# Fewer, wider filler products in the opening of a fused attention and gated feed-forward kernel

## The chip, the cores and the metric

The kernel runs on one core of a Trainium2 chip. The metric is device time in microseconds (us) of one execution; the kernel before takes 227.95 us (median of 8 runs, 227.79 to 228.54).

## The reference, cut to what matters

For each of 8 batches there are x (8 heads, 512 rows, 64 columns) and a state (8 heads, 32 rows, 64 columns). They attend to each other, the results are put together to 544 rows of 512 per batch, and all rows go through a gated feed-forward layer.

```python
scores  = scale * x @ state.T;  a  = softmax(scores);  xread = a  @ state   # per batch, per head
scores2 = scale * state @ x.T;  a2 = softmax(scores2); sread = a2 @ x
x = concatenate([xread, sread], axis=2)        # heads side by side: (8*544, 512)
gate = maximum(x @ w_gate, 0)                  # (512, 1536)
val  = x @ w_val
out  = (gate * val) @ w_out                    # (1536, 512)
```

## The kernel before, in words

Matrix products are in bf16 with sums in fp32. The kernel never forms xread: since xread = a @ state, the product x @ w_gate is a @ (state @ w_gate). So for each batch b it makes U = state @ w_gate and state @ w_val (128 x 1536 for each half of the heads and each weight), and then multiplies U by the transposed probabilities ANS.

The work of a batch runs over these helpers. The name that the program text uses for each stands in front.

- **dx, dw, do, ds, df** load x, the gate and value weights, the output weight, the rest of the state and a raw x. All of these are issued on POOL's queue (L95 to L112, L418). A `dw.w.lo.n` loads columns lo to lo+n of weight w (0 gate, 1 value).
- **stc, stT, sto**: the state is converted (L119, L122), transposed on TensorE (L127) and copied out of PSUM to stT (L131).
- **xc, xT, xo** (batch 0) and **xT2, xo2** (batches 1 and 2): x is converted to xb (L144), transposed on TensorE (L167, L171, L184) and copied to xT (L175, L187). The first half of batch 0 comes in fp32 over SyncE's and ScalarE's queues and is converted on VectorE; its other half and batches 1 and 2 are converted by POOL's DMA on the way.
- **sc, ex, nr, nx**: scores (L198), exponential (L205), sum and reciprocal (L211, L213), scaling to a_sn (L217).
- **aT, ao**: a_sn is transposed (L233) and copied to ANS (L247).
- **c, co** and **u, uo**: pieces of U, on TensorE (L289) and copied out (L309, L299).
- **gv, re, mu**: gate and value for 128 columns (L314), relu (L338), product (L342) to h_sb.
- **o, of**: output products (L351), copy and store (L359).
- **sr, sn**: the other attention's read (L262).

The code is scheduled by hand (`manual_schedule`): each engine does its instructions in the order of the calls. For the opening, some 55 us, that order is a text, `program` (L440 on), of words such as `xT2.1.1@2`: the helper, its arguments, and after @ the numbers of the PSUM banks that it writes. After it, loops over g (batch and block of 128 columns) issue gv, relu, mult and output pieces, with the work of later batches hung on fixed places.

PE (TensorE) has words of its own in the text, `spin`: filler products whose result, in bank 7 (`warm_ps`), nothing reads. Their operands are 512 zero columns of hs_sb, which is not used until the end; VectorE clears them first (L394).

```python
def spin(n, cols=512):
    for i in range(n):
        nc.tensor.matmul(warm_ps[:, 0:cols], warm[:, 0:128], warm[:, 0:cols], start=True, stop=True)
```

There are nine groups in the opening: ahead of stT.0, of xT.0.1, of sc.0.0, of xT.0.2, of sc.0.1, of xT2.1.1, of sc.1.0, of c.1.0.128 and of c.0.128.128. A filler waits for no engine but for the first clearing; it lies in PE's order, so what follows it can't start until it is through. The first wide products, gv.0.0, come after the last group.

Of the kernel before, what the change touches and what calls it, by code (L numbers as in the profile page):

```python
# [16 lines left out]
def kernel(  # L17
# [52 lines left out]
    stT = const.tile([128, B, NJ, 64], BF16, name="stT")  # L70
# [5 lines left out]
    xf, xb, xT, e_sn, a_sn, ANS, U, hsb, sr_sb = {}, {}, {}, {}, {}, {}, {}, {}, {}  # L76
# [360 lines left out]
             "c": c_unit, "co": c_out, "u": u_unit, "uo": u_out, "gv": gv, "re": relu, "mu": mult, "o": out_part,  # L437
             "of": fin_x, "xn": x_next, "xp": x_pad, "sr": sr_mm, "sn": sr_norm}
    program = """
    dx.1.0.2 dx.1.1.2 stc.0.0.act stc.0.1.dve spin.23.128 stT.0@0 xc.0.0.dve dw.0.0.128 sto.0.act dw.1.0.128 on  # L440
    xc.0.1.dve spin.16.128 xT.0.1@1 dw.0.128.128 xT.0.0@2 xo.0.1.dve xo.0.0.act dw.1.128.128 spin.13.128 sc.0.0@3
    dw.0.256.256 ex.0.0 spin.4.128 xT.0.2@4 xT.0.3@5 xo.0.2.dve dw.1.256.256 xo.0.3.act nr.0.0 spin.13.128 sc.0.1@0
    dw.0.512.256 xT2.1.0@1 ex.0.1 nx.0.0 xo2.1.0.act nr.0.1 dw.1.512.256 spin.8.128 xT2.1.1@2 xo2.1.1.act spin.2.128
    sc.1.0@3 dw.0.768.256 nx.0.1 ex.1.0 dw.1.768.256 spin.10.128 c.1.0.128@45 c.0.0.128@01 co.1.0.128.0.dve aT.0.1@2
    co.0.0.128.0.act aT.0.0@3 co.1.0.128.1.dve co.0.0.128.1.act dw.0.1024.256 sc.1.1@4 ao.0.1.dve ao.0.0.act nr.1.0
    ex.1.1 dw.1.1024.256 spin.7.128 c.0.128.128@05 gv.0.0@12 co.0.128.128.1.act nr.1.1 co.0.128.128.0.act nx.1.0.pool
    re.0.0 gv.0.1@34 mu.0.0 re.0.1 nx.1.1.pool c.1.128.128@50 mu.0.1 co.1.128.128.1.act c.0.256.256@12
    co.1.128.128.0.act c.1.256.256@30 dw.0.1280.256 co.0.256.256.0.dve co.0.256.256.1.act aT.1.1@5 aT.1.0@4
    co.1.256.256.0.act co.1.256.256.1.dve dw.1.1280.256 gv.0.3@21 ao.1.1.act ao.1.0.dve dx.2.0.1 re.0.3 gv.0.2@30
    mu.0.3 ds re.0.2 c.1.512.256@54 mu.0.2 gv.1.2@21 co.1.512.256.1.act co.1.512.256.0.act do.0.6 c.0.512.256@30  # L450
    re.1.2 gv.1.5@45 co.0.512.256.0.dve xp.1 co.0.512.256.1.act mu.1.2 re.1.5 gv.1.3@23 mu.1.5 re.1.3 gv.1.1@04
    do.6.12 mu.1.3 re.1.1 c.1.768.256@15 xp.0 mu.1.1 gv.1.4@23 co.1.768.256.0.act co.1.768.256.1.act c.0.768.256@04
    re.1.4 gv.1.0@15 co.0.768.256.0.dve co.0.768.256.1.act df.3 mu.1.4 re.1.0 gv.1.6@20 mu.1.0 re.1.6 gv.0.4@41 mu.1.6
    re.0.4 gv.0.6@35 mu.0.4 re.0.6 gv.1.7@20 mu.0.6 re.1.7 c.0.1024.256@41 c.0.1280.256@35 mu.1.7 co.0.1024.256.0.act
    xT2.2.0@2 stc.1.0.pool co.0.1024.256.1.act co.0.1280.256.1.dve xT2.2.1@0 stc.1.1.pool co.0.1280.256.0.act
    xo2.2.0.dve gv.0.5@41 stc.3.0.pool stc.3.1.pool xo2.2.1.dve re.0.5 stc.2.1.pool gv.0.10@53 stc.2.0.pool mu.0.5
    re.0.10 stT.1@2 gv.0.9@40 mu.0.10 sto.1.act re.0.9 sc.2.1@1 gv.0.8@52 ex.2.1 mu.0.9 re.0.8 nr.2.1 gv.0.11@34
    re.0.11 mu.0.8 gv.0.7@10 nx.2.1.pool mu.0.11 re.0.7 sc.2.0@5 o.0.0@6 mu.0.7 ex.2.0 nr.2.0 c.1.1280.256@32
    c.1.1024.256@14 co.1.1280.256.1.act u.2.1.1024@50 o.0.1 co.1.1024.256.0.dve co.1.1024.256.1.act nx.2.0.pool
    uo.2.1.1024.1.dve uo.2.1.1024.0.act o.0.2 co.1.1280.256.0.act u.2.0.0@21 xn.3 of.0.0.dve u.2.1.0@45 uo.2.0.0.1.act  # L460
    u.2.1.512@03 uo.2.1.0.0.dve o.0.3@7 uo.2.1.0.1.act uo.2.0.0.0.dve uo.2.1.512.0.act aT.2.0@1 aT.2.1@4
    uo.2.1.512.1.dve ao.2.0.act o.0.4 ao.2.1.act o.0.5 gv.2.1@50 of.0.1.act re.2.1 gv.1.10@23 mu.2.1 re.1.10
    gv.1.11@14 mu.1.10 re.1.11 gv.2.3@50 mu.1.11 re.2.3 gv.2.2@23 mu.2.3 re.2.2 u.2.0.1024@14 u.2.0.512@50 mu.2.2
    uo.2.0.1024.1.act sr.0@2 o.0.6@6 uo.2.0.512.1.act uo.2.0.512.0.dve sn.0 gv.1.9@34 uo.2.0.1024.0.dve re.1.9
    gv.1.8@05 mu.1.9 re.1.8 gv.2.0@21 mu.1.8 re.2.0 o.0.7 mu.2.0 o.0.8 o.0.9@7 of.0.2.dve sr.1@3 sn.1 xp.2 xp.3
    """
    for word in program.split():
        word, _, banks = word.partition("@")
# [101 lines left out]
```

## Time and profile before

| | |
|---|---|
| median of 8 runs | 227.95 us |
| the profiled execution's own time | 227.82 us |
| span of its profile | 226.0 us |
| TensorE products busy | 220.6 us, 98% of the span |
| VectorE, ScalarE, GpSimd busy | 57%, 55%, 23% |
| fillers (L430) | 96 products, 9.3 us busy, 261 ns mean |
| gv products (L314) | 384, 96.6 us |
| output products (L351) | 372, 94.5 us |

The span is what the profiler saw of the engines' work; what lies around it makes the time longer by 1.8 us. PE is TensorE's product, PEld its weight load, DVE VectorE, ACT ScalarE, POOL GpSimd, SP SyncE. A product's duration contains the time that it takes to drain through the array, so products that overlap have a mean above their spacing: a row of output products says 379 ns, and they follow each other every 216 ns. Start times are in us from the start of the span. A DMA's time to landing counts from its issue.

### The profile page before, as it was taken

To read this page: it belongs to the slowest core of one execution; us is meant where nothing else is said; L and a number is where in the kernel's file an instruction comes from. 1 tells how busy PE (TensorE), PEld (TensorE's weight loads), DVE (VectorE), ACT (ScalarE), POOL (GpSimd) and SP (SyncE) were. 2 spreads that over 40 slices of the span, in tenths; PEclk is the share of its full clock that TensorE was granted. 3 is DMA by queue.
4 is the path that set the end of the run, shared out by engine and by line. 5 is a ranking of instruction groups with operands and counts; after the bars stand their busy time and mean duration, and the time that the engine had idled before them with its cause. 6 is when DMAs were issued, how large, how long until landed. Compare 5 with 4: busy or idle time off the path is not lost.

```text
span 226.0 us, 5017 instructions
## 1 busy us (share of the span) xinstructions
PE 220.6 (98%) x2040; PEld 110.8 (49%) x2040; DVE 128.4 (57%) x226; ACT 124.8 (55%) x236; POOL 53.1 (23%) x58
## 2 busy tenths in 40 slices
PE   7999999999999999999999999999999999999994
PEld 6964454444445444434434444344444445666543
DVE  3477888757478648763877467656855443222100
ACT  4489878865366654755556455555555444322221
POOL 8699838503333060006000600000000000000000
PEclk9999999999999999999999999999999999999999
DMA  6999999070719921691179113611311111111132
GB/s 147 178 195 196 213 227 273 27 186 3 208 70 133 252 85 46 139 278 50 49 97 260 69 62 75 142 46 46 96 46 49 46 48 46 48 51 76 62 94 95
DMA packets 37800, 25.50 MB, mean 113 GB/s; under 512 B 18864, under 2 KB 33200, under 8 KB 37776
## 3 DMA queue, kind: packets, MB, share of 16 engines
q1 hardware_dynamic: 24912, 16.85, 27.6%
q0 software_dynamic: 11968, 7.47, 21.4%
q10 hardware_dynamic: 896, 0.85, 1.3%
q8 instruction: 16, 0.26, 0.5%
q14 instruction: 8, 0.07, 0.1%
HBM read 18.35 MB, written 8.91 MB: 121 GB/s over the span
## 4 chain that ended last, share of the span: by engine, by line
PE 96%; DMA 1%; ACT 0%; issue 0%; DVE 0%; DVEq 0%; ACTq 0%
PE o_ps L351 38%; PE gv_ps L314 38%; PE gv_ps L331 5%; PE up L289 4%; PE warm_ps L430 2%; PE upc L289 2%; PE sc_ps L198 2%; PE sr_ps L262 1%; DMA st_f<-in_state_dram 1%; PE o_ps L377 1%; PE xT_ps L184 1%; PE aT_ps L233 1%; PE stT_ps L127 1%; PE srT_ps L275 0%; PE xT_ps L167 0%
## 5 line engine op out<-in xcount | busy, mean ns | idle before, releaser
L314 PE MATMUL gv_ps<-ans,U 128*128 128x512 bf16 x384 | 96.6, 380 | 0.0
L351 PE MATMUL o_ps<-wo_sb,h_sb 128*128 128x512 bf16 x372 | 94.5, 379 | 0.0
L342 DVE TENSOR_TENSOR h_sb<-gv_ps,g_sb 128x512 bf16<-128x512 f32 x96 | 65.3, 688 | 42.2 <-ACT g_sb L338 41.0
L338 ACT ACTIVATE g_sb<-gv_ps 128x512 bf16<-128x512 f32 (+1 forms) x108 | 63.0, 584 | 47.0 <-PE gv_ps L314 32.4
L351 PEld LDWEIGHTS <-h_sb 128*128 128x128 bf16 x372 | 36.0, 98 | 41.0 <-issue 0.7
L314 PEld LDWEIGHTS <-U 128*128 128x128 bf16 x384 | 34.8, 98 | 41.3 <-issue 4.2
L359 ACT COPY o_sb<-o_ps 128x512 f32<-128x512 f32 x29 | 17.0, 586 | 20.7 <-PE o_ps L351 20.7
L299 DVE CAST U<-up 128x512 bf16<-128x512 f32 x36 | 23.2, 685 | 5.3 <-PE up L289 5.2
L299 ACT CAST U<-up 128x512 bf16<-128x512 f32 x36 | 19.4, 592 | 10.1 <-PE up L289 10.1
L140 POOL CAST xb<-xf 128x1024 bf16<-128x1024 f32 x10 | 10.3, 1060 | 52.4 <-DMA xf<-in_x_dram 42.7
L254 POOL COPY xa<-xb 128x2048 bf16<-128x2048 bf16 (+1 forms) x9 | 15.3, 1711 | 13.9 <-issue 7.0
L211 DVE TENSOR_REDUCE cs<-e_sn 128x16 f32<-128x512 bf16 x16 | 10.9, 683 | 8.6 <-ACT e_sn L205 8.6
L342 DVE TENSOR_TENSOR hs_sb<-gv_ps,g_sb 128x256 bf16<-128x256 f32 x12 | 5.1, 425 | 15.3 <-PE gv_ps L331 10.5
L205 ACT ACTIVATE e_sn<-sc_ps 128x512 bf16<-128x512 f32 x16 | 9.6, 601 | 5.6 <-PE sc_ps L198 5.6
L430 PE MATMUL warm_ps<-hs_sb 128*128 128x128 bf16 x96 | 9.3, 261 | 1.5 <-DVE hs_sb L394 1.2
L309 ACT CAST U<-upc 128x512 bf16<-128x512 f32 (+1 forms) x20 | 9.5, 530 | 1.7 <-PE upc L289 1.6
L289 PEld LDWEIGHTS <-stT 64*32 64x32 bf16 x512 | 4.9, 89 | 10.6 <-issue 10.1
L430 PEld LDWEIGHTS <-hs_sb 128*128 128x128 bf16 x96 | 7.7, 121 | 2.0 <-DVE hs_sb L394 1.2
L217 DVE TENSOR_TENSOR a_sn<-e_sn,rc 128x512 bf16<-128x512 bf16 x12 | 8.3, 692 | 0.6
L331 PE MATMUL gv_ps<-br,wg_sb 128*128 128x256 bf16 x48 | 7.2, 273 | 0.0
L331 PE MATMUL gv_ps<-br,wv_sb 128*128 128x256 bf16 x48 | 7.2, 273 | 0.0
L289 PE MATMUL up<-wg_sb,stT 64*32 64x512 bf16 x144 | 7.2, 386 | 0.0
(64 smaller groups left out, 133.9 us busy)
## 6 DMA issues: line engine op xcount, KB each, us to landing
out_dram<-o_sb SPq DMA_DIRECT2D x31, 256.0 KB, 2.3
xf<-in_x_dram SPq DMA_DIRECT2D x4, 1024.0 KB, 6.2
wo_sb<-in_moe_w_out_dram POOLq DMA_DIRECT2D x2, 768.0 KB, 15.4
wg_sb<-in_moe_w_gate_dram POOLq DMA_DIRECT2D x5, 256.0 KB, 8.6
wv_sb<-in_moe_w_val_dram POOLq DMA_DIRECT2D x5, 256.0 KB, 9.2
xf<-in_x_dram POOLq DMA_DIRECT2D x1, 1024.0 KB, 16.0
xb<-in_x_dram POOLq DMA_DIRECT2D x3, 256.0 KB, 7.3
xb<-in_x_dram POOLq DMA_DIRECT2D x1, 512.0 KB, 12.0
```

Source lines behind the costliest of these rows:

```text
L140: copy[eng](out=xb[b][:, :, hs].rearrange("p c h d -> p h c d"), in_=xf[b][:, hs])
L211: nc.vector.reduce_sum(out=cs, in_=e_v, axis=AX.X)
L254: nc.gpsimd.tensor_copy(out=v[:, hs:hs + src.shape[1]], in_=src)
L289: nc.tensor.matmul(dst[parity][32 * j:32 * j + 32], stT[r:r + 64, b, j, 32 * parity:32 * parity + 32], wsb[r:r + 64, j, lo:lo + n], start= ...
L299: copy[eng](out=U[b][:, w, kc, lo:lo + 512], in_=held["u", b, w, lo][kc])
L314: nc.tensor.matmul(ps[w], U[b][:, w, kc, f0:f0 + 128], ANS[b][:, kc].rearrange("p c t -> p (c t)"), start=(kc == 0), stop=(kc == NK - 1))
L331: nc.tensor.matmul(ps[w][:, 0:nt], wsb[:, j, f0:f0 + 128], br[:, j].rearrange("p b n -> p (b n)"), start=(j == 0), stop=(j == NJ - 1))
L338: nc.scalar.activation(out=g_sb[:, 0:n], in_=ps[0][:, 0:n], func=AF.Relu)
L342: nc.vector.tensor_tensor(out=dst, in0=ps[1][:, 0:n], in1=held["g", b, jf][:, 0:n], op=ALU.mult)
L351: nc.tensor.matmul(held["o", b, tsub], src[:, jf, tsub * 128:(tsub + 1) * 128], wo_sb[:, jf], start=(jf == 0), stop=(jf == NF - 1))
L359: copy[eng](out=o_sb, in_=held["o", b, tsub])
L430: nc.tensor.matmul(warm_ps[:, 0:cols], warm[:, 0:128], warm[:, 0:cols], start=True, stop=True)
```

## The change

Only numbers in the program text change, at nine places. Each group of fillers of 128 columns becomes a group of 512 columns (the helper's default); the group of two ahead of sc.1.0 goes. No other word changes its place, its arguments or its banks.

```diff
-    ... stc.0.1.dve spin.23.128 stT.0@0 xc.0.0.dve dw.0.0.128 sto.0.act dw.1.0.128 on
+    ... stc.0.1.dve spin.7 stT.0@0 xc.0.0.dve dw.0.0.128 sto.0.act dw.1.0.128 on
-    xc.0.1.dve spin.16.128 xT.0.1@1 dw.0.128.128 xT.0.0@2 xo.0.1.dve xo.0.0.act dw.1.128.128 spin.13.128 sc.0.0@3
+    xc.0.1.dve spin.3 xT.0.1@1 dw.0.128.128 xT.0.0@2 xo.0.1.dve xo.0.0.act dw.1.128.128 spin.3 sc.0.0@3
-    dw.0.256.256 ex.0.0 spin.4.128 xT.0.2@4 xT.0.3@5 xo.0.2.dve dw.1.256.256 xo.0.3.act nr.0.0 spin.13.128 sc.0.1@0
+    dw.0.256.256 ex.0.0 spin.1 xT.0.2@4 xT.0.3@5 xo.0.2.dve dw.1.256.256 xo.0.3.act nr.0.0 spin.3 sc.0.1@0
-    dw.0.512.256 xT2.1.0@1 ex.0.1 nx.0.0 xo2.1.0.act nr.0.1 dw.1.512.256 spin.8.128 xT2.1.1@2 xo2.1.1.act spin.2.128
+    dw.0.512.256 xT2.1.0@1 ex.0.1 nx.0.0 xo2.1.0.act nr.0.1 dw.1.512.256 spin.2 xT2.1.1@2 xo2.1.1.act
-    sc.1.0@3 dw.0.768.256 nx.0.1 ex.1.0 dw.1.768.256 spin.10.128 c.1.0.128@45 c.0.0.128@01 co.1.0.128.0.dve aT.0.1@2
+    sc.1.0@3 dw.0.768.256 nx.0.1 ex.1.0 dw.1.768.256 spin.2 c.1.0.128@45 c.0.0.128@01 co.1.0.128.0.dve aT.0.1@2
-    ex.1.1 dw.1.1024.256 spin.7.128 c.0.128.128@05 gv.0.0@12 co.0.128.128.1.act nr.1.1 co.0.128.128.0.act nx.1.0.pool
+    ex.1.1 dw.1.1024.256 spin.2 c.0.128.128@05 gv.0.0@12 co.0.128.128.1.act nr.1.1 co.0.128.128.0.act nx.1.0.pool
```

## The prediction

> **What bounds the kernel now.** Read in this order. The page's first parts: TensorE (PE) is busy 98% of a span of 226.0 us, and the chain that ended last is 96% PE. So only time in which PE holds no useful work can be won. The list of PE's waits has four entries, all in the first 18 us:
>
> ```profile
> PE warm_ps L430 <- DVE hs_sb L394: 1.2, 1, 1.2
> PE stT_ps L127 <- ACT st_b L119: 0.4, 1, 0.4
> PE warm_ps L430 <- issue: 0.4, 1, 0.4
> PE upc L289 <- ACT U L309: 0.2, 1, 0.2
> ```
>
> PE waits so little because fillers stand in for waits. The timeline of PE (start, duration of the run of instructions, line, count) shows where; the duration includes the drain of the last product, so a group's cost is the distance to the next start.
>
> ```profile
> 1.18 2.63 PE L430 MATMUL warm_ps<-hs_sb 128*128 128x128 bf16 x23 [1.18 <-DVE hs_sb L394]
> 4.20 0.61 PE L127 MATMUL stT_ps<-id,st_b 128*128 128x128 bf16 x4 [0.39 <-ACT st_b L119]
> 4.59 1.91 PE L430 MATMUL warm_ps<-hs_sb 128*128 128x128 bf16 x16
> 6.30 1.06 PE L167 MATMUL xT_ps<-id,xb 128*128 128x128 bf16 x8
> 7.16 1.09 PE L430 MATMUL warm_ps<-hs_sb 128*128 128x128 bf16 x13
> 8.08 0.40 PE L198 MATMUL sc_ps<-stT,xT 128*128 128x64 bf16 x8
> ...
> 11.38 0.64 PE L184 MATMUL xT_ps<-id,xb 128*64 128x128 bf16 x16
> ...
> 14.08 0.28 PE L430 MATMUL warm_ps<-hs_sb 128*128 128x128 bf16 x2
> 14.73 0.45 PE L430 MATMUL warm_ps<-hs_sb 128*128 128x128 bf16 x5 [0.37 <-issue]
> 15.11 0.25 PE L289 MATMUL upc<-wg_sb,stT 64*32 64x128 bf16 x8
> 15.35 1.90 PE L314 MATMUL gv_ps<-ans,U 128*128 128x512 bf16 x8
> ```
>
> Two things are to be seen. The 16 fillers take 6.30-4.59 = 1.71 us, 107 ns each, and the transposes behind them 107 ns too; from about 7.5 us on fillers start 57 ns apart. The page's row of the granted clock says 9 tenths or more throughout, so it doesn't record this; the spacing does. And the fillers overrun what they cover: the transposes at 6.30 read xb, which DVE finished at 5.23 (its casts: 4.11 for 1.12 us). PE is 1.0 us late by its own fillers. Later the inputs are closer. ACT's timeline and the DMA issues of two windows (duration last, from issue to landing):
>
> ```profile
> 12.06 1.01 ACT L187 COPY xT<-xT_ps 128x1024 bf16<-128x1024 bf16 x1
> 14.06 0.60 ACT L247 COPY ans<-aT_ps 128x512 bf16<-128x512 bf16 x1
> ```
>
> ```profile
> xb<-in_x_dram POOLq DMA_DIRECT2D x1, 256.0 KB, 7.8
> ```
>
> The last is the second half of batch 1: issued at 3.16, landed at 10.96, read at 11.38. ACT is busy without a gap from 10.94 to 15.17.
>
> **The change, step by step.** 96 fillers of 128 columns become 23 of 512. A 512 one has no row; by the cold 128 row it is 4 x 107 = 427 ns, and warm 216 ns, which the o_ps products of 512 show (12 in 2.75 us, less the 0.38 of the last, over 11). Removed are 73 products and 73 weight loads; nothing else moves.
> First group: 23 x 107 = 2.46 becomes 7 x 427 = 2.99, to 4.17. The state's transposes wait for ACT until 4.20 anyway: cost 0 to 0.02; the cover is st_b.
> Second: 16 x 107 = 1.71 becomes 3 x 427 = 1.28: the transposes start at 5.87, 0.43 earlier, still behind the fillers.
> Third: from 6.73 until ACT's copy of xT ends (7.56). Three fillers: 427, then one that the clock's rise at about 7.53 cuts (400), then 216: scores at 7.77, against 8.08. Gain now 0.31.
> Fourth: one for 0.22 in place of four at 57: xT.0.2 at 8.30. The tail of batch 0 was issued at 1.43 and took 6.5: 7.93, so it is there. Gain 0.33.
> Fifth: 3 x 216 = 0.65 for 13 x 57 = 0.74; ACT's copy ends at 9.57, scores at 9.61, the next transposes at 9.93; their data landed at 2.41 + 7.3 = 9.71. Gain 0.33.
> Sixth: 2 x 216 = 0.43 for 0.46, then xT2.1.1 wanted at 11.02 and landed at 10.96: I take 11.05. Gain 0.33. Here cover ends: no filler taken away here can win more, and ACT's second copy starts at 11.74 instead of 12.06.
> Seventh, dropped: 0.12; sc.1.0 waits on ACT until about 11.75.
> Eighth: 0.43 for 0.57: the first c units at 12.53; wv landed at 4.61 + 7.8 = 12.41.
> Ninth: 0.43 for 7 x 57 = 0.40, but with the 0.37 "issue" stall (0.53 from the end of the second filler) out of the way c.0.128.128 runs at 14.17, its weight in at 6.34 + 7.6 = 13.94. gv.0.0 then waits for ACT's ans copy, 14.66 - 0.28 = 14.38. It starts at about 14.45 instead of 15.35: **0.90 ahead**.
>
> **Where it is given back.** Three things behind it do not move with PE.
> First, DVE's mult frees the bank of c.0.256.256, about 16.7 against 17.4: gain 0.65 to 0.7 for that unit; its wv weight landed at 8.23 + 8.3 = 16.53, in time.
> Second, the stall. It comes after 223 products and as many loads, with no wait in sight. The instruction queue's packets of 16 KB start at 12.0, 18.5 and 25.5 us. The Trainium skill ("Runtime: NRT & Kernel Launch", Instruction fetch mechanics) says that code comes in 16 KiB blocks of 256 instructions and that a boundary is mostly hidden; it gives PE room for 2048, so by the page PE would not stall after 446. The row shows one that isn't hidden. If 512 is the boundary (446 and some 66 unlisted), its block was asked for at the boundary before. From the stall's end at 14.73 to the next packet is 3.8; 12.0 - 3.8 = 8.2 for the first request; 14.73 - 8.2 = 6.5 us from request to use. In the changed kernel the same count comes 73 products later: the request during xT2.1.1, about 11.3, use at 17.6 to 17.9, in the middle of c.1.256.256, which PE would reach at 17.1 to 17.4. What follows it (aT.1.1) then starts at 17.6 to 18.0 instead of 18.33: gain 0.35 to 0.7. By the page's rule nothing would be lost here, 0.85 stays. I take 0.55, by the row.
> Third, data. Batch 2 was issued at 19.00 and took 12.0: 31.0, and PE's transposes of it start at 31.65, so about 0.6 survives. The tighter place comes next. POOL converts the rest of the state as soon as it has landed, and PE's transposes of it (stT.1) come close behind:
>
> ```profile
> 32.12 5.43 POOL L122 TENSOR_SCALAR st_b<-st_f,odd 128x256 bf16<-128x256 f32 x6 [4.87 <-DMA st_f<-in_state_dram]
> 34.44 0.39 PE L127 MATMUL stT_ps<-id,st_b 128*128 128x128 bf16 x4
> ```
>
> Two of six conversions are done at 32.12 + 2 x 0.91 = 33.95, and PE can follow at about 34.0: **0.44 ahead and no more**, if the state lands when it did. POOL would issue both loads up to 0.37 earlier (its scale of a_sn starts at 15.06, behind its own weight issues, instead of 15.46); but the DMA engines are 90% busy up to 39 us, so a load issued earlier waits longer, and I leave the landing. With a full credit for the issue the end is 0.6 to 0.8. After 40 us PE has no waits and DMA is nearly idle: the advance goes to the end.
> Sum against the profiled execution: 227.82 - 0.44 = 227.38, and the 0.55 of the code block lies under it. The median of the runs is 0.13 above that execution (the runs lie in two groups, 227.8 to 228.0 and 228.4 to 228.5), so 227.5; a small part of the earlier issue, 0.05, gives **227.45**, a gain of 0.50.
>
> **The clock.** "TensorE: Matmul & The Clock Gate", Part 1, says that the clock doubles after one busy window of about 3.4 us, that windows run free, and that the transition is near 4 us of activity. Here it came 6.3 us after the first filler. The page warns too that transposes may not count as activity, which speaks against fewer fillers. In 4.1 to 7.5 I count 1.71 + 0.37 of fillers before and 1.28 + 0.80 after: the same. If the closed gap at 3.8 to 4.2 lets the clock rise at about 4.1, the transposes start at 5.28 instead of 5.87, but the landings at 7.93, 9.71 and 10.96 bind then and the sum gains under 0.05. If it rises one window later, 10.9, the fillers of both kernels double.
>
> **Rivals.** (1) *The gain is eaten* (0.10): loads or POOL hold the stretch from 16 to 34 us so firmly that less than 0.3 is left. For it: margins of 0.06 to 0.2 us at six landings of my schedule. Against it: each is met in this trace. Time 227.65 to 228.4. (2) *Slower* (0.20): the code block. Its request moves to 11.3, where DMA moves 190 GB/s against 175 before. Below a latency of 7.0 us (18.3 - 11.3) it decides for the change, above it each us is a us lost. The next block was not missed until PE reached it near 22, 7.3 after its request, so no more is excluded than that; at 7.8 the time is 228.8. (3) *Most of it stays* (0.28): no block stall, and the loads of batch 2 and the state land with their earlier issue: 0.6 to 0.85, so 227.1 to 227.35.
>
> **How the numbers follow.** The likeliest case, the caps at 31 and 34 us, has 0.42 and a gain of 0.35 to 0.55, so 227.4 to 227.6. What a measurement here can tell is 0.2%, 0.46 us, which lies inside that case: I count 0.17 of it as faster. Faster is 0.17 + 0.28 = 0.45, same 0.25 + 0.10 = 0.35, slower 0.20. The range goes from 226.95 (all stays, with 0.15 of scatter) to 228.5 (all is eaten, with the upper group of runs), which leaves out the worse part of rival 2.
>
> **What would show it.** Right: transposes of xT.0.1 near 5.9; gv.0.0 near 14.45; no "issue" gap near 14, one near 17.5; xT2.2.0 close behind its landing at 31, stT.1 close behind POOL. Wrong: fillers at 216 ns from 4 us on, gv.0.0 still at 15, or PE waiting on DMA before 20 us. My weakest step is the code block, since a stall of one trace carries it.

## The result, and the profile after

The changed kernel takes **226.74 us** (median of 11 runs, 226.05 to 227.71) against 227.94 for the kernel before (31 runs). The ratio is 0.995, 95% interval 0.9933 to 0.9967: 0.5% faster, clear of no change. The forecast was 227.45 us with a range of 226.95 to 228.5. Its direction held; the gain was 1.2 us in place of 0.5, and the time lies 0.2 us below the range.

The profiled execution took 227.55 us with a span of 225.8, and is not a typical one: nine of the eleven runs lie between 226.05 and 226.80. What it lost is seen at the end of this section. The timeline of PE in the opening, changed kernel:

```profile
1.17 3.17 PE L430 MATMUL warm_ps<-hs_sb 128*128 128x512 bf16 x7 [1.17 <-DVE hs_sb L394]
4.16 0.61 PE L127 MATMUL stT_ps<-id,st_b 128*128 128x128 bf16 x4
4.56 1.41 PE L430 MATMUL warm_ps<-hs_sb 128*128 128x512 bf16 x3
5.81 0.61 PE L167 MATMUL xT_ps<-id,xb 128*128 128x128 bf16 x8
6.25 0.81 PE L430 MATMUL warm_ps<-hs_sb 128*128 128x512 bf16 x3
7.09 0.41 PE L198 MATMUL sc_ps<-stT,xT 128*128 128x64 bf16 x8
...
10.74 0.64 PE L184 MATMUL xT_ps<-id,xb 128*64 128x128 bf16 x16 [0.29 <-DMA xb<-in_x_dram]
...
13.21 0.40 PE L198 MATMUL sc_ps<-stT,xT 128*128 128x64 bf16 x8
13.44 0.59 PE L430 MATMUL warm_ps<-hs_sb 128*128 128x512 bf16 x2
13.96 0.25 PE L289 MATMUL upc<-wg_sb,stT 64*32 64x128 bf16 x8
14.03 0.24 PE L289 MATMUL upc<-wv_sb,stT 64*32 64x128 bf16 x8
14.20 1.92 PE L314 MATMUL gv_ps<-ans,U 128*128 128x512 bf16 x8
...
16.94 0.30 PE L289 MATMUL upc<-wv_sb,stT 64*32 64x256 bf16 x8 [0.33 <-DMA wv_sb<-in_moe_w_val_dram]
```

The state's transposes follow the first fillers without a pause. The eight transposes at 5.81 are already fast: their starts span 0.61 less 0.22 us, 56 ns apart, so the clock rose near 5.75 us, not 7.5. PE now waits for batch 1's second half (10.74) and the wv weight (16.94); the stall near 14 us is gone. gv.0.0 starts at 14.20, 1.15 us earlier than before. The scores at 13.21 (sc.1.1) show how this is made up. In the kernel before they stood here:

```profile
13.85 0.40 PE L198 MATMUL sc_ps<-stT,xT 128*128 128x64 bf16 x8
```

So 0.64 us of the 1.15 is there ahead of the last fillers, and 0.51 comes from there to gv.0.0, where the stall was. The wait for the wv weight at 16.94 then takes a part back: by ScalarE's starts the advance falls from 1.12 to 0.76 us there.

POOL's conversions of the state, and PE's transposes of it, changed kernel:

```profile
31.28 5.43 POOL L122 TENSOR_SCALAR st_b<-st_f,odd 128x256 bf16<-128x256 f32 x6 [3.79 <-DMA st_f<-in_state_dram]
33.67 0.39 PE L127 MATMUL stT_ps<-id,st_b 128*128 128x128 bf16 x4
```

PE passes this place 0.77 us earlier than before (34.44), where the prediction allowed 0.44: the state had landed 0.8 us earlier, and PE doesn't wait here. The advance holds until 65 us, and then 0.5 of it goes. DVE's scaling of batch 3's probabilities there, kernel before:

```profile
63.80 0.69 DVE L217 TENSOR_TENSOR a_sn<-e_sn,rc 128x512 bf16<-128x512 bf16 x1
```

DVE's timeline there, changed kernel:

```profile
63.02 1.44 DVE L217 TENSOR_TENSOR a_sn<-e_sn,rc 128x512 bf16<-128x512 bf16 x1
64.39 1.27 DVE L342 TENSOR_TENSOR h_sb<-gv_ps,g_sb 128x512 bf16<-128x512 f32 x2
```

POOL's timeline at the same place, changed kernel:

```profile
62.89 2.48 POOL L140 CAST xb<-xf 128x1024 bf16<-128x1024 f32 x2 [3.71 <-DMA xf<-in_x_dram]
```

And PE's:

```profile
65.72 1.02 PE L314 MATMUL gv_ps<-ans,U 128*128 128x512 bf16 x4 [0.19 <-DVE h_sb L342]
```

Batch 4's x landed, POOL began its cast at 62.89, and DVE's scaling beside it took 1.44 us in place of 0.69. Everything behind it on DVE is late, and PE's bank with it. From there to the end PE is 0.26 us ahead of before, not 0.77.

### The profile page after: what moved, and what is told of

The parts are those of the page before. It is cut to its first block, busy times and chain, and to the rows that moved or that the text cites. A ratio compares the mean times of both kernels' runs of the same rounds, so it can differ in the third digit from the quotient of the medians.

```text
span 225.8 us, 4871 instructions
## 1 busy us (share of the span) xinstructions
PE 220.3 (98%) x1967; PEld 105.4 (47%) x1967; DVE 129.1 (57%) x226; ACT 124.9 (55%) x236; POOL 53.3 (24%) x58
## 4 chain that ended last, share of the span: by engine, by line
PE 90%; DMA 4%; POOL 3%; DVE 1%; issue 1%; DVEq 0%; POOLq 0%
PE o_ps L351 38%; PE gv_ps L314 37%; PE gv_ps L331 5%; PE up L289 4%; DMA wv_sb<-in_moe_w_val_dram 4%; PE upc L289 1%; PE sr_ps L262 1%; PE o_ps L377 1%; PE sc_ps L198 1%; POOL wg_sb L108 1%; POOL xb L418 1%; POOL wv_sb L108 1%; DVE h_sb L342 1%; PE xT_ps L184 0%; PE aT_ps L233 0%
## 5 line engine op out<-in xcount | busy, mean ns | idle before, releaser
L289 PEld LDWEIGHTS <-stT 64*32 64x32 bf16 x512 | 4.9, 89 | 11.8 <-issue 11.5
L430 PE MATMUL warm_ps<-hs_sb 128*128 128x512 bf16 x23 | 8.4, 486 | 1.2 <-DVE hs_sb L394 1.2
L217 DVE TENSOR_TENSOR a_sn<-e_sn,rc 128x512 bf16<-128x512 bf16 x12 | 9.1, 754 | 0.6
L198 PEld LDWEIGHTS <-xT 128*128 128x128 bf16 x128 | 5.7, 98 | 3.8 <-ACT xT L175 0.7
```

Of the source, the lines that this page charges most:

```text
L289: nc.tensor.matmul(dst[parity][32 * j:32 * j + 32], stT[r:r + 64, b, j, 32 * parity:32 * parity + 32], wsb[r:r + 64, j, lo:lo + n], start= ...
```

## The experiments

Three theories stood against each other. A: the gain is the overrun taken from groups 2 to 9. B: the first group closes a gap, the clock rises earlier, and that is the gain. C: the stall near 14 us goes with the number of products. Beside them two questions from the profile were open: what the meeting at 63 us is worth, and why the state's landing did not hold PE back.

Below, "advance" is how much earlier than in the first profile of the kernel before the same ScalarE instruction starts; "landing" is that of batch 1's second half, to about 0.05 us. Where two advances are given they are those at 36 to 62 us and from 68 us to the end; one number means that nothing was lost between.

| kernel | gv.0.0 | landing | clock rose near | advance | median, ratio to before (95%) |
|---|---|---|---|---|---|
| before | 15.35 | 10.95 | 7.6 | 0 | 227.94 |
| before, again | 15.72 | 10.74 | 7.7 | -0.37 | 228.19, one run |
| changed | 14.20 | 10.74 | 5.75 | 0.77, then 0.26 | 226.74, 0.9950 (0.9933-0.9967) |
| changed, again | 13.95 | 10.44 | 5.55 | 0.87, then 0.37 | 226.94, 0.9964 (0.9946-0.9982) |
| wide_same | 14.77 | 10.45 | 7.0 | 0.48 | 227.61, 0.9988 (0.9969-1.0006) |
| narrow | 14.29 | 10.05 | 5.95 | 1.06 | 227.29, 0.9974 (0.9957-0.9991) |
| g1_only | 15.11 | 10.35 | 6.4 | 0.24 | 227.73, 0.9983 (0.9960-1.0006) |
| rest_only | 14.24 | 10.45 | 6.25 | 1.08, then 0.54 | 227.53, 0.9987 (0.9970-1.0004) |
| g2_one | 15.00 | 11.54 | 7.2 | 0.32 | 227.54, 0.9979 (0.9956-1.0002) |
| no_fillers | 15.19 | 10.85 | 15.1 | 0.00, then -0.49 | 228.17, 1.0015 (0.9991-1.0038) |
| first_three | 13.88 | 10.44 | 6.8 | 1.28, then 0.80 | 227.23, 0.9960 (0.9940-0.9981) |
| early_x4 | 14.16 | 10.34 | 6.2 | 1.15 | 226.89, 0.9955 (0.9938-0.9972) |
| early_x4, again | 14.13 | 10.44 | 6.1 | 1.19 | 226.94, 0.9954 (0.9934-0.9974) |
| three_early | 13.94 | 10.15 | 7.2 | 0.76 | 227.04, 0.9955 (0.9938-0.9972) |
| late_issue | 14.09 | 10.44 | 6.3 | 1.17, then 0.60 | 227.10, 0.9973 (0.9957-0.9989) |

The clock's rise is read from the spacing of fillers and transposes (512 columns 427 ns or 216 ns apart, 128 columns 107 or 56), to about 0.1 us.

**The same columns in fewer products.** Each group keeps its columns; 96 products become 33.

```diff
- ... spin.23.128 ... spin.16.128 ... spin.13.128 ... spin.4.128 ... spin.13.128 ... spin.8.128 ... spin.10.128 ... spin.7.128
+ ... spin.5 spin.3.128 ... spin.4 ... spin.3 spin.1.128 ... spin.1 ... spin.3 spin.1.128 ... spin.2 ... spin.2 spin.2.128 ... spin.1 spin.3.128
```

> The kernel before with exactly its filler columns in each group, but 33 products in place of 96 (512 wide, the rest 128). If the number of products matters through the code stall (63 fewer): no stall near 14 us, gv.0.0 at 14.7 to 14.9 in place of 15.35, 0.4 to 0.5 us faster than before. If only the columns matter: a stall or a wait of the same length is found elsewhere and the time is within 0.2 us of before.

PE's timeline ahead of gv.0.0, this kernel:

```profile
13.82 0.40 PE L198 MATMUL sc_ps<-stT,xT 128*128 128x64 bf16 x8
14.27 0.33 PE L430 MATMUL warm_ps<-hs_sb 128*128 128x128 bf16 x3
14.53 0.25 PE L289 MATMUL upc<-wg_sb,stT 64*32 64x128 bf16 x8
...
14.77 1.99 PE L314 MATMUL gv_ps<-ans,U 128*128 128x512 bf16 x8
```

Up to the scores at 13.82 it stands where the kernel before stood (13.85). There is no stall (the wide filler of the group has no record; it fills the 0.2 us ahead of 14.27), gv.0.0 comes 0.58 us earlier, and 0.48 of it stays to the end. So in its trace the number of products alone is worth half a microsecond, as expected. The timed runs don't confirm it: their ratio is worth 0.3 us, and its interval includes no change.

**The new columns in narrow products.** The changed kernel with four products of 128 for each of 512.

```diff
- ... spin.7 ... spin.3 ... spin.3 ... spin.1 ... spin.3 ... spin.2 ... spin.2 ... spin.2
+ ... spin.28.128 ... spin.12.128 ... spin.12.128 ... spin.4.128 ... spin.12.128 ... spin.8.128 ... spin.8.128 ... spin.8.128
```

> The changed kernel with each filler of 512 columns replaced by four of 128: the same columns, 92 products in place of 23. Theories A and B: as the changed kernel within 0.3 us, 226.5 to 227.0. Theory C: the stall near 14 us is back, 0.3 to 0.5 us of idle TensorE ahead of gv.0.0, which starts at 14.6 to 15.0; the time is 227.2 or more if nothing behind it hides the stall.

PE's timeline of its last group, and the last weight load in that group:

```profile
13.28 0.83 PE L430 MATMUL warm_ps<-hs_sb 128*128 128x128 bf16 x8
```

```profile
13.88 0.10 PEld L430 LDWEIGHTS <-hs_sb 128*128 128x128 bf16 x1 [0.22 <-issue]
```

The stall is there, after the seventh filler of the group: the 223rd product again. It is 0.22 us, shorter than expected, and gv.0.0 comes at 14.29 all the same. 1.06 us of advance stays to the end. It is faster than before by its interval; whether narrow fillers cost anything against wide ones with these columns can't be told (0.9974 against 0.9950 and 0.9964, intervals overlap).

**The first group alone.** The kernel before with the gap ahead of the state's transposes filled.

```diff
- ... spin.23.128 stT.0@0
+ ... spin.28.128 stT.0@0
```

> The kernel before with its first filler group alone changed, 28 of 128 columns in place of 23, so that TensorE has no gap before the state's transposes. Theory A (the gain is the overrun of groups 2 to 9, and when the clock rises is a matter of its phase): the transposes of xT.0.1 stay near 6.3 us, gv.0.0 near 15.3, and the time within 0.3 us of before. Theory B (the closed gap makes the clock rise earlier, and that is the gain): fillers 57 ns apart from 5.8 us on in place of 7.5, and 0.5 us or more faster. Theory C (the stall marked issue near 14 us goes with 73 fewer products): the stall stays, 0.4 us, and comes five products earlier.

PE's timeline around the stall, this kernel:

```profile
13.57 0.31 PE L198 MATMUL sc_ps<-stT,xT 128*128 128x64 bf16 x5
14.29 0.26 PE L198 MATMUL sc_ps<-stT,xT 128*128 128x64 bf16 x3 [0.41 <-issue]
```

Five fillers more, and the stall comes five products earlier, in the middle of a group of scores. The advance is 0.24 us, in an execution whose clock rose at 6.4 in place of 7.6; the timed ratio includes no change. Theory C's forecast for the place of the stall is met to the product.

**All but the first group.**

```diff
- ... spin.7 stT.0@0
+ ... spin.23.128 stT.0@0
```

> The changed kernel with the first group as before, 23 of 128 columns; all else changed. Theory A: as the changed kernel, 226.5 to 227.0 us as median, gv.0.0 near 14.3. Theory B: the clock rises at 7.5 us or later, gv.0.0 at 14.5 or later, the time 227.3 or more. Theory C: 57 products fewer than before, so no stall near 14 us.

The trace speaks for theory A (gv.0.0 at 14.24, 1.08 us of advance at 60 us), and against B: with 0.67 us of idle PE ahead of the state's transposes the clock rose at 6.25, as early as with a closed gap. The timed runs do not confirm A: 227.53, half a microsecond above the expected median. They suggest that the closed gap is worth something in executions that were not profiled. Over all traces the clock rose at 6.25 to 7.7 with the gap (four traces) and at 5.55 to 7.2 without it (ten with the first group filled): they overlap, and this stays open. In the timed runs none of the three partial changes (wide_same, g1_only, rest_only) is clear of no change; narrow, which has all the new columns, and the changed kernel are. How the gain divides among the theories is therefore read from the traces only.

**One filler where three overran.**

```diff
- ... spin.3 xT.0.1@1
+ ... spin.1 xT.0.1@1
```

> The changed kernel with one filler of 512 columns in place of three ahead of the first x transposes, whose input is ready some 0.6 us before they start. If the landing of batch 1's second half, at 10.1 to 11.0 us, is what the opening ends on: the transposes start near 5.2, gv.0.0 within 0.1 us of the changed kernel's 14.2, the time within 0.2 us of it. If the overrun still counts: gv.0.0 0.3 to 0.6 us earlier and the time 0.3 us less. If the clock needs these fillers: it rises [...]later, and the time is 0.5 us or more above the changed kernel.

PE's timeline, this kernel:

```profile
5.69 1.03 PE L167 MATMUL xT_ps<-id,xb 128*128 128x128 bf16 x8 [0.25 <-DVE xb L144]
...
11.54 0.64 PE L184 MATMUL xT_ps<-id,xb 128*64 128x128 bf16 x16
...
15.00 1.92 PE L314 MATMUL gv_ps<-ans,U 128*128 128x512 bf16 x8
```

The fillers had become shorter than the wait: PE waited for xb until 5.69. Nothing was won. In this execution the data landed late, at 11.54, and gv.0.0 came 3.46 us after; in the changed kernel's first profile it was 14.20 - 10.74 = 3.46 too. Where PE is there first, the landing sets gv.0.0. The timing is inconclusive.

**No fillers, and the first three groups only.**

```diff
- ... spin.7 ... spin.3 ... spin.3 ... spin.1 ... spin.3 ... spin.2 ... spin.2 ... spin.2
+ (none)                                                        # no_fillers
+ ... spin.7 ... spin.3 ... spin.3                              # first_three
```

> The changed kernel with all fillers left out. If they are there only for the clock[...]: TensorE runs at half its rate until about 18 us, transposes 107 ns apart, the first gv products 427 ns apart, 1 to 3 us slower than the changed kernel. If the clock would rise anyway from the real work: no slower than the changed kernel, gv.0.0 near 14.2, since landings and ScalarE set it.

> The changed kernel with its first three filler groups only (13 products), the later ten left out. If the fillers are needed only until the clock has risen (5.4 to 7.5 us in the traces so far): it stays up, gv.0.0 between 13.9 and 14.3, the time within 0.2 us of the changed kernel. If TensorE's pauses of up to 0.7 us let it fall: transposes 107 ns apart again after 8 us and at least 0.5 us slower than the changed kernel.

PE's timeline without fillers:

```profile
7.95 1.06 PE L171 MATMUL xT_ps<-id,xb 128*64 128x128 bf16 x16
10.18 1.92 PE L184 MATMUL xT_ps<-id,xb 128*64 128x128 bf16 x32
13.45 1.04 PE L233 MATMUL aT_ps<-id,a_sn 128*128 128x128 bf16 x8
```

Sixteen transposes take 1.06 us in place of 0.64: the clock stays low until about 15.1 us, just ahead of the first gv products. Yet the whole costs only 1.2 us against the changed kernel timed beside it (228.17 against 226.94), and against the kernel before nothing that can be measured. By the traces, what that kernel's fillers won by the clock their overrun and the stall took back (gv.0.0 at 15.19 without fillers, 15.35 with them). With the first three groups alone the clock stays up after its rise at 6.8, although PE pauses five times for more than 0.15 us, up to 0.3; its trace is the fastest of all up to 62 us. The ratio is the changed kernel's. Its median, 227.23, is 0.3 higher against a slower before (228.14), so the ten later fillers do nothing that was measured.

**Batch 4's load earlier.** It is issued right behind batch 3's transposes, not ten microseconds later.

```diff
- ... xn.3 of.0.0.dve ...
+ ... xn.3 d4 of.0.0.dve ...          # d4: x_dma(4, (nc.sync,))
-    at(2, 4, x_dma, 4, (nc.sync,))
```

> The changed kernel with batch 4's load of x issued on SyncE's queue right after batch 3's transposes, some 10 us earlier. In the changed kernel's profile GpSimd's cast of this batch began at 62.9 us and VectorE's scaling beside it took 1.44 us in place of 0.69, and TensorE lost 0.5 us there. If that meeting is what separates its executions of 227.6 from those of 226.7, no execution here is above 227.2, the cast starts before 61 us, and the median is 226.5 to 226.8. If it is not, the executions spread as those of the changed kernel do, 226.0 to 227.7.

> The changed kernel with batch 4's load early, once more. If the meeting of GpSimd's cast with VectorE's scaling costs its executions 0.5 us each time it happens: median 226.5 to 226.9, and the share of executions above 227.4 below the changed kernel's one in four. If the spread comes from the opening: as the changed kernel, 226.9 with a quarter above 227.4.

> The same with batch 4's load issued after batch 3's transposes as well. If both hold: 226.6 to 226.9 as median and fewer executions above 227.4 than the changed kernel has; no scaling of 1.4 us in the profile.

POOL's timeline, early_x4:

```profile
58.73 2.02 POOL L140 CAST xb<-xf 128x1024 bf16<-128x1024 f32 x2
```

In all three traces the cast is through before the scaling, the scaling takes 0.69 us, and the whole advance reaches the end. In the others the two meet by chance. In six of them the scaling was first, in g1_only by 0.03 us (63.56 against the cast's 63.59): it took 0.69 us, and the cast 2.23 to 2.55 in place of 2.02. Where the cast began first (the changed kernel twice, rest_only, no_fillers, first_three, late_issue), the scaling took 1.40 to 1.50 us and PE lost 0.48 to 0.57. That is how the Trainium skill has it ("SBUF — State Buffer", SBUF: two separate sides): the port pair of VectorE and GpSimd is locked by whoever starts first, for its whole instruction, and the other waits.

The forecast of the timing failed. Four of 17 runs and five of 22 lie above 227.4 (the changed kernel: nine of 33), and the medians are the changed kernel's. So the meeting explains the profiled executions, each of them matched by its own time (227.55 and 227.46 with it, 226.67 and 226.63 without it), but not the spread of the others. No version was found that beats the changed kernel.

**The kernels once more.**

> The kernel before once more, for its trace. If the landings of its first profile were a draw of that execution: the second half of batch 1 lands before 10.9 us and the rest of the state before 31.9 us with the same issue times, and the clock rises at another time than 7.5 us. If they belong to this kernel: within 0.2 us of 10.95, 31.98 and 7.5. The stall after 223 products near 14 us is there in both cases.

> The changed kernel once more, timed beside the others. If VectorE's scaling for batch 3 waits for GpSimd's cast (1.4 us in place of 0.69) its advance falls by 0.5 us at 65 us as in its first profile; if it doesn't, the advance of about 1.0 us stays to the end and the profiled execution is near 226.7. The second half of batch 1 lands between 10.0 and 11.0 us; the clock rises between 5.8 and 7.6. Median 226.5 to 227.0.

PE's timeline around the stall, kernel before, second trace:

```profile
14.22 0.28 PE L430 MATMUL warm_ps<-hs_sb 128*128 128x128 bf16 x2
15.10 0.45 PE L430 MATMUL warm_ps<-hs_sb 128*128 128x128 bf16 x5 [0.60 <-issue]
```

The stall is at the same product with 0.60 us in place of 0.37, and the clock rose at the same time; the landings moved by 0.2 us. The changed kernel's second trace has the meeting again. It shows besides that a landing can cap the advance: the state landed at 31.6, later than in the first trace, and PE's transposes of it come close behind POOL.

```profile
33.56 0.40 PE L127 MATMUL stT_ps<-id,st_b 128*128 128x128 bf16 x4
```

The advance was 0.98 us ahead of this place and is 0.87 behind it.

**The issue of the loads, delayed.** Only POOL waits a little ahead of the last weight loads: 1.0 us of memsets on an unused tile.

```diff
- ... c.1.256.256@30 dw.0.1280.256
+ ... c.1.256.256@30 dl dw.0.1280.256   # dl: three nc.gpsimd.memset(delay, 0.0)
```

> The changed kernel with three small memsets of an unused tile on GpSimd, some 0.7 to 1.0 us together, ahead of the load of the gate weight's columns 1280 to 1535; all loads behind it are issued that much later, as in the kernel before (17.3 to 17.9 us in place of 16.5 to 16.7). If a load's landing follows its issue here: the rest of the state lands at 31.3 to 32.0 us as in the traces of the kernel before, TensorE's transposes of it can't start before 33.3 to 34.0, and where that is later than it would come, its advance falls to 0.4 to 0.9 us; 0.1 to 0.4 us slower than the changed kernel. If a load issued later only waits less, as the prediction had it: the state lands at 30.1 to 31.5 us and the time is the changed kernel's.

POOL's timeline, this kernel:

```profile
16.55 1.04 POOL L439 MEMSET delay<- 128x256 bf16 x3
17.54 0.81 POOL L109 DMA_DIRECT2D wg_sb<-in_moe_w_gate_dram  x1
...
30.71 5.44 POOL L123 TENSOR_SCALAR st_b<-st_f,odd 128x256 bf16<-128x256 f32 x6 [3.61 <-DMA st_f<-in_state_dram]
```

The loads are issued as late as in the kernel before, and the state lands at 30.65, the fifth earliest of 15. In this trace a load issued later only waits less, and the timed ratio, 0.9973, overlaps the changed kernel's. What tells a landing is another landing: in 14 of 15 traces the state lands 6.3 to 6.4 us after the last weight issued ahead of POOL's scaling (dw.1.1024), wherever POOL issued it. The exception is the one trace that the prediction had: 24.61 and 31.98, 7.4 us apart. There the next weight (dw.0.1280) landed 2.9 us after dw.1.1024; in the other 14 it came 1.3 to 1.4 us after it.

## Why the prediction was wrong, point by point

- *The state's landing, "0.44 ahead and no more".* This step failed, by its size. That such a landing can cap the advance is right: it took 0.1 us in the changed kernel's second trace. The claim that an earlier issue doesn't move it held in late_issue. But 31.98 us was one execution's landing, and the latest of 15. The other 14 lie between 30.05 and 31.77 and let PE pass 0.2 to 1.9 us earlier than that. In the changed kernel's first trace it was 31.2 and held nothing back; the advance there, 0.77 us, had been set at 17 us by the wv weight, which the prediction had at 16.53, "in time", and which PE got at 16.94. The advances at 60 us of the traces with the changed program's fillers, 0.77 to 1.19, have the size of the timed gain: 1.2 us in the first timing, 0.8 by the second ratio (0.0036 x 228.05).
- *The code block, "use at 17.6 to 17.9 ... I take 0.55".* The first half is right: a stall at 223 products is a matter of the count; it moved with five more fillers, went with 63 fewer, and is worth about 0.5 us. The second half failed. The changed kernel's traces show no stall at 17.5 us; the transposes of a_sn start 0.9 us earlier (17.40 against 18.33), not 0.35 to 0.7. One error is in the working: at 8.2 us the kernel before is at its products 65 to 72, but 11.3 us is put at xT2.1.1, the products 80 to 95 of the changed kernel. Its products 65 to 72 lie in xT2.1.0, near 10.2 in the prediction's schedule; 6.5 us later is 16.7, before PE gets there. Besides, the packets' starts were read in steps of half a microsecond; finer, they are 12.5, 18.7 and 25.5. In the four traces with the stall, it ends 2.2 to 2.5 us after such a packet starts (12.5 and 14.73 before, 12.7 and 15.10 in its second trace, 11.8 and 14.29 in g1_only, 11.5 and 13.88 in narrow). The changed kernel's packet started at 14.6, so by this its code was there at 16.8 to 17.1, and PE's 224th weight load starts at 17.1. The rival on the slower side falls with it.
- *The overrun.* Right in its place, but small: 0.33 us was forecast at xT2.1.1 (11.05), and 0.64 came (10.74 against 11.38), since the data landed at 10.74 and not at 10.96 and the clock had risen at 5.75, so that PE was there first. gv.0.0, forecast at 14.45, came at 14.20.
- *The clock.* Forecast at 7.5 and found at 5.5 to 7.2 in the kernels with the first group filled. An earlier rise bought little: three_early, at 7.2, still has gv.0.0 at 13.94. Why it comes where it comes isn't settled.
- *"After 40 us PE has no waits ... the advance goes to the end."* Right for most, and wrong in an execution with the meeting at 63 us, which takes 0.5 us.
- *The rival "most of it stays" (0.28)* was the nearest case, by luck: its condition, an earlier landing, was met, but by late_issue the reason given, an earlier issue, was not it. Its 227.1 to 227.35 still lies above the 226.74 measured.

## What to carry to other kernels

A landing time read from one execution is a draw; before it is used as a cap, look at how it hangs on other landings, and widen the range by its scatter. Fillers cost twice: by the time that they overrun their wait, and by their count, where PE stalls after a certain number of products; wide ones keep the array busy with a quarter of the instructions. And an advance is only safe when the chance meetings downstream (here a cast and a scaling 40 us later) are looked at too.

## What the runs showed of the hardware that was not expected

- TensorE stalled after the same product, the 223rd (446 listed instructions), in four traces with narrow fillers: 0.37, 0.60, 0.41 and 0.22 us. The instruction packets of 16 KB fit the Trainium skill's account of code loading in blocks ("Runtime: NRT & Kernel Launch", Instruction fetch mechanics), but not its room of 2048 instructions for TensorE; that the stall ends 2.2 to 2.5 us after a packet's start in all four speaks for the block's arrival as its cause, but no run moved a packet alone, so this is argued, not shown.
- The clock rose between 4.4 and 6.5 us after the first filler, with PE 87 to 100% busy in between, and stayed up through pauses of up to 0.6 us (three_early, ahead of 11.46).
- Without any filler the clock stayed low until about 15 us, although transposes, scores and small products kept PE busy for 66 to 100% of each 2 us from 6 us on.
- VectorE's scaling of 0.69 us took 1.40 to 1.50 where GpSimd's cast had begun first; where the scaling was first, it took 0.69, and the cast 2.23 to 2.55 us for 2.02.
